# A recurrent attention block and a maxout FFN in one kernel: query and score parts of y made transposed from the fifth chunk on, one weight load for keys and queries in odd units

## The chip, the core and the metric

One core of one Trainium2 chip runs the whole program. The metric is the device time of one execution in microseconds. Before the change three runs took 515.86, 516.76 and 520.91 us; the median is 516.76.

## What is computed

Two blocks follow each other. The first is a delta rule, a recurrence over 768 tokens with a 48x48 state for each of 4 batches and 8 heads; the second is a feed-forward network (FFN) with a maximum over three products. Cut to what matters:

```python
q, k, v: (4, 8, 768, 48); beta: (4, 8, 768)
k_n = k / (norm(k) + 1e-6)
for t in range(768):
    y[:, :, t] = q[t] @ state
    v_old = state.T @ k_n[t]
    state = state + beta[t] * outer(k_n[t], v[t] - v_old)
x = y.transpose(0, 2, 1, 3).reshape(3072, 384)
h = maximum(maximum(x @ w1, x @ w2), x @ w3)      # w: (384, 768)
out = h @ w_out                                   # (768, 384)
```

## The kernel before

**Tiles.** The 768 tokens are cut into 12 chunks of 64. A chunk has two units (g = 0, 1), each with two of the four batches; unit n belongs to chunk n // 2. Within a unit the two batches (bb) stand on partitions 0 to 63 and 64 to 127. Two chunks of all four batches make 512 tokens, one FFN group m (0 to 5). Everything is fp32, and the trace has two records for each such matmul.

**A chunk's steps.** For each unit `gram` (L395) multiplies the transposed keys with the keys (`at`) and with the queries (`pt`, masked to the causal part). The score matrix of 64x64 needs a triangular solve; `solve` (L498) does it for 32-token blocks of two chunks at once, on VectorE, with a round trip through DRAM (`at_d`, `x_bl`, `y_d`, `ut`); `join_z` and `join_u` put the halves together. Then `old_k` (L738) subtracts keys times state from the values (`p_k`), `new` (L753) applies the solved triangle (`p_u`, copied to `u` by ScalarE), `step` (L771) adds to the state (`p_s`, `st`), `old_q` (L747) makes queries times state (`p_q`, copied to `qs` by ScalarE) and `to_y` (L793) adds the scores times `u` (`p_y`) on VectorE. Every one of these small products is 32 matmuls on the four 64x64 quadrants of TensorE, so 64 records.

**From y to x.** The FFN needs x with its 384 features on partitions. For chunks 0 to 3 `to_x` (L807) transposes y on TensorE. For chunks 4 to 11 `y_blocks` (L833) writes y to DRAM by two transfers from SP's queue, `read_y` (L844) reads it back into the tile `qall` by four, with another order, and `turn_y` (L857) turns 32x32 blocks on VectorE into `xt`.

**The order is written out by hand.** `ffn(m)` (L903) is a generator that yields after each product. At its yields the loop at the end (L1173) issues steps of the recurrence for group m + 1 and loads for later groups, by a table of names and digits:

```python
LINKS = {
    0: "k0 q0 t0 L3", 1: "t1", 2: "g0 g1 t2", 3: "z0 z1 d0 d1", 4: "j0 j1 t3 V0",
    5: "g2 g3 p1", 6: "u0 N0", 7: "V1 N1", 8: "s0 y0 N2", 9: "x0", 10: "k1 q1",
    11: "u1 w0", 13: "y1 x1 s1", 14: "X0 w1", 16: "P0", 17: "X1 K0 K1 K2 K3",
}
```

Digits 0 and 1 of k, q, u, s, y, x, w and X name the even and the odd chunk of the group. A yield of the first twelve is one hidden product (`p_h`, 3 matmuls); from yield 12 on it is half an output product (`p_o`). So the recurrence of chunks 4 to 11 is made within passes 1 to 4 over the FFN. The first pass, m = 0, has a table of its own (`FIRST`, `EARLY_LINKS`) with chunks 1 to 3 in it, the units 8 to 11 of `gram`, and the conversion of the weights (`mant`, `up` on ScalarE, VectorE and POOL). The solve of group m + 2 begins at yield 8 of pass m, for m up to 3, and goes on in small portions, three steps a yield. Each engine works through its own queue in the order recorded; a step that waits holds up what stands behind it on that engine.

**PSUM.** `p_h`, `p_m` and `p_o` take turns in two buffers (`ffn`), all the small products in three buffers of two banks (`two`). A p_h stage of yield i can begin when the buffer of yield i - 2 is read: by ScalarE's ReLU for the even yields, by VectorE's maximum (L928) for the odd ones.

Of the kernel before, what the change touches and what calls it, by code (L numbers as in the profile page):

```python
# [9 lines left out]
FP32 = mybir.dt.float32  # L10
# [4 lines left out]
ALU = mybir.AluOpType  # L15

C = 64
# [6 lines left out]
def kernel(  # L24
# [31 lines left out]
    nc = tc.nc  # L56

    B, H, S, D = q.shape
    NCH = S // C
    DM = H * D  # L60
    DFF = moe_w1.shape[1]
    KT = DM // 128
    FT = DFF // 128
    NP = H // 2
# [18 lines left out]
    def ps_two(name):  # L83
        return psum.tile([128, 2, 512], FP32, name=name, tag="two", bufs=3)
# [5 lines left out]
    qall = const.tile([128, NQ, H, DP], FP32, name="qall")  # L90
# [18 lines left out]
    def rows(bb):  # L109
        return slice(C * bb, C * (bb + 1))  # L110

    def dims(par):
        return slice(DP * par, DP * par + D)
# [196 lines left out]
    def by_par(t):  # L310
        return t.rearrange("p (j two) x -> p two j x", two=2)
# [83 lines left out]
    def gram(n, parts=(0, 1), queues=one_queue, copy=nc.scalar.copy, later=False):  # L395
        kqt, g = kqts[n], n % 2
        p_g = ps_two("p_g")

        whole = len(parts) == 2 and not g
        for j in range(NP):  # L400
            for par in range(2):
                for bb in range(2):
                    kq = kqt[dims(par), j, bb ^ g]
                    for i in (0,) if whole else parts:
                        c0 = j * 128 + i * C
                        nc.tensor.matmul(  # L406
                            p_g[
                                rows(bb ^ (g * i)), par, c0 : c0 + C * (1 + whole)
                            ],
                            kq[:, 0],  # L410
                            kq if whole else kq[:, i],
                        )
        p_v = p_g.rearrange("p two (j i t) -> p two j i t", j=NP, i=2)
        if 1 in parts:
            pt = pts[n] = square("pt")
            if later:
                copy(by_par(pt), p_v[:, :, :, 1])
            else:
                masked(pt, p_v[:, :, :, 1])
        if 0 not in parts:  # L420
            return
        at = ats[n] = square("at")
        copy(by_par(at), p_v[:, :, :, 0])
        if queues:
            to_dram(n, queues)
# [178 lines left out]
    def both(name, w, bufs=1):  # L604
        return work.tile([128, 2, H, w], FP32, name=name, bufs=bufs)
# [110 lines left out]
                negate[bb](u12[block(bb), :, span(hs)], p_v[bb][block(bb)], -1.0)  # L716


    xts, rhss, qss, us, yts = {}, {}, {}, {}, {}

    def heads(t):
        return t.rearrange("p g (j two) d -> p two (g j) d", two=2)

    def times_state(kqt, i, name):
        p_b = ps_two(name)
        for j in range(NP):
            for g in range(2):
                for par in range(2):
                    for bb in range(2):
                        c0 = (g * NP + j) * D  # L730
                        nc.tensor.matmul(  # L731
                            p_b[rows(bb), par, c0 : c0 + D],
                            kqt[g][dims(par), j, bb ^ g, i],
                            st[dims(par), bb ^ g, g, j],
                        )
        return p_b[:, :, 0 : H * D].rearrange("p two (x d) -> p two x d", d=D)

    def old_k(c):  # L738
        rhss[c] = vts.pop(c)
        if c:  # L740
# [3 lines left out]
                out=rhs, in0=rhs, in1=times_state(kqt, 0, "p_k"), op=ALU.subtract  # L744
            )

    def old_q(c):  # L747
        kqt = [kqts[2 * c + g] for g in range(2)]
        if c:
            qs = qss[c] = both("qs", D)  # L750
            nc.scalar.copy(heads(qs), times_state(kqt, 1, "p_q"))

    def new(c):  # L753
        rhs = rhss.pop(c)
# [38 lines left out]
    def to_y(c):  # L793
        u = us[c]
        pt = [pts.pop(2 * c + g) for g in range(2)]
        y = yts[c] = both("y", D)
        for hs, p_v, copy in heads_of(c, "p_y", D):
            for i, h in enumerate(hs):
                for bb, g in TILES:
                    r = rows(bb ^ g)  # L800
                    nc.tensor.matmul(p_v[rows(bb), g, i], pt[g][r, h], u[r, g, h])  # L801
            if c:
                nc.vector.tensor_tensor(out=y, in0=qss.pop(c), in1=p_v, op=ALU.add)
            else:
                copy(y[:, :, span(hs)], p_v)

# [21 lines left out]
        if c:  # L828
            nc.scalar.copy(xt, of)

    yds, yqs = {}, {}

    def y_blocks(c):  # L833


        y = yts.pop(c)
        y_d = yds[c] = dram.tile([32, 2, 4, DM], FP32, name="y_x")
        for g in range(2):
            nc.sync.dma_start(
                out=y_d[:, g].rearrange("t b x -> b t x"),  # L840
                in_=y[:, g].rearrange("p h d -> p (h d)"),
            )

    def read_y(c):  # L844
        y_d = yds.pop(c)
        y_q = yqs[c] = qall.rearrange("p i h d -> p (i h d)")[
            :, 768 * (c % 2) : 768 * (c % 2 + 1)
        ].rearrange("p (b x) -> p b x", x=96)
        for a in range(4):
            nc.sync.dma_start(  # L850
                out=y_q[32 * a : 32 * (a + 1)],
                in_=y_d[:, :, :, 96 * a : 96 * (a + 1)].rearrange(
                    "t g b x -> t (g b) x"
                ),
            )

    def turn_y(c):  # L857
        m, cc = divmod(c, 2)
        if m not in xts:
            xts[m] = work.tile([128, KT, TOK], FP32, name="xt")  # L860
        nc.vector.transpose(
            out=xts[m][:, :, cc * 256 : (cc + 1) * 256].rearrange(
                "p t (b x) -> p b t x", x=32
            ),
            in_=yqs.pop(c).rearrange("p b (x t) -> p b t x", t=KT),
        )

    def less_first(f):
# [34 lines left out]
    def ffn(m):  # L903
        xt = xts[m]
        hs = {}

        def hidden(f, lo, w):
            if f not in hs:
                hs[f] = square("h").rearrange("p h c -> p (h c)")
            h = hs[f][:, lo : lo + w]  # L910
            for i in range(m > 0, 3):
                p_h = ps_ffn([128, TOK], "p_h")[:, 0:w]
                for t in range(KT):
                    nc.tensor.matmul(  # L914
                        p_h,
                        w_sb[i][:, t, f * 128 : (f + 1) * 128],
                        xt[:, t, lo : lo + w],
                        start=(t == 0),
                        stop=(t == KT - 1),
                    )  # L920
                if i == 0:
                    nc.scalar.copy(h, p_h)
                elif m and i == 1:
                    nc.scalar.activation(  # L924
                        out=h, in_=p_h, func=mybir.ActivationFunctionType.Relu
                    )
                else:
                    nc.vector.tensor_tensor(out=h, in0=h, in1=p_h, op=ALU.max)  # L928
                yield


        early = FT // 2 if m == 0 else 0
        for lo in (0, TOK // 2):
            for f in range(early):
                yield from hidden(f, lo, TOK // 2)
        for f in range(early, FT):
            yield from hidden(f, 0, TOK)
        for i in range(4):
            cc, g = divmod(i, 2)
            p_o = ps_ffn([128, DM], "p_o")  # L940
            last = slice(i * 128, (i + 1) * 128)
            terms = [(hs[f][:, last], wo_sb[:, f]) for f in range(FT)]
            if m:
                terms += [(xt[:, t, last], w_sb[0][:, t, 0:DM]) for t in range(KT)]
            for n, (stays, moves) in enumerate(terms):
                nc.tensor.matmul(  # L946
                    p_o, stays, moves, start=(n == 0), stop=(n == len(terms) - 1)
                )
                if m and n == 4:
                    yield  # L950
            o_sb = work.tile([128, DM], FP32, name="o_sb")
            nc.scalar.copy(o_sb, p_o)  # L952
            for bb in range(2):
                tok0 = (2 * bb + g) * S + (2 * m + cc) * C
                nc.sync.dma_start(out=out[tok0 : tok0 + C, :], in_=o_sb[rows(bb)])
            yield


# [79 lines left out]
    for _ in range(2):  # L1038
# [25 lines left out]
    LINKS = {  # L1064
# [3 lines left out]
    }  # L1068
    EARLY_LINKS = {
# [11 lines left out]


    RECURS = dict(
        z=join_z, j=join_u, k=old_k, q=old_q, u=new, s=step, y=to_y, x=to_x,
        e=halves_z, f=halves_u, d=turn_t1,
    )
    MADE = dict(V=load_v, P=prep_values)
# [79 lines left out]
            turn_first((2 * (i - 27), 2 * (i - 27) + 1))  # L1167


    RECURS.update(x=y_blocks, w=read_y, X=turn_y, p=prep_values)  # L1170
    UNIT.update(t=turn_blocks, K=lambda n: load_k(n, (nc.gpsimd, nc.gpsimd)))
    MADE.update(V=lambda c: load_v(c, nc.gpsimd))
    for m in range(1, GROUPS):  # L1173
# [42 lines left out]
```

## Time and profile before

The profiled execution took 523.32 us (span from first to last instruction 521.3 us, mean granted TensorE clock 0.966), against the median of 516.76 us of the three runs.

| what (line) | engine | count | mean |
|---|---|---|---|
| p_h, 128x512 (L914) | TensorE | 414 records | 606 ns, overlapped |
| y addition, 128x768 (L803) | VectorE | 11 | 952 ns |
| state addition, 48x768 (L789) | VectorE | 14 | 951 ns |
| 128x1024 product of the solve (L538) | VectorE | 4 | 1224 ns |
| mask of pt, 128x512 (L390) | VectorE | 20 | 689 ns |
| transpose to xt, 128x768 (L861) | VectorE | 8 | 1224 ns |
| copy of p_q, 128x768 (L751) | ScalarE | 11 | 800 ns |
| copy of 128x1024 from PSUM (L335) | ScalarE | 4 | 1009 ns |
| y to DRAM (L839) | SP's queue | 16 | 192 KB each |
| y back from DRAM (L850) | SP's queue | 32 | 96 KB each, 2.6 us to landing |

Matmuls overlap in their pipeline, so a stage's time is read from its start to the start of the next stage, not from the means of its records. "Idle before, with a releaser" names what ended an engine's wait. Passes over the FFN begin at 46, 162, 246, 322, 395 and 463 us.

### The profile page before, as it was taken

The numbers are of one execution on the slowest core, as the hardware profiler recorded it, in microseconds if no ns is written. First come the engines' busy times: TensorE is split into PE (matmuls) and PEld (weight loads), VectorE is DVE, ScalarE is ACT, GpSimd is POOL, SyncE is SP. The second block draws the span as 40 slices with busy tenths as digits, with TensorE's granted clock in tenths as the row PEclk, the third lists the DMA queues.
The fourth block names the chain that finished last, engine by engine and source line by source line (L and its number), as shares of the span: only waits on it lengthen the run. The fifth ranks groups of instructions, "written<-read, shape, count | busy, mean of one in ns | idle before, by whom it ended". The sixth has DMA issues, their size and how long they took to land.

```text
span 521.3 us, 18005 instructions
## 1 busy us (share of the span) xinstructions
PE 496.0 (95%) x7836; PEld 306.0 (59%) x7836; DVE 306.0 (59%) x689; ACT 163.3 (31%) x302; POOL 192.6 (37%) x317
## 2 busy tenths in 40 slices
PE   7578799998999999999999999999999999999996
PEld 6467688755565555665555565555655555654453
DVE  5888969867996430998642987635896321111100
ACT  4575755883422242201243101252101411011000
POOL 6435462783391926670665680503130000000000
PEclk9956989999999999999989999999999999999999
DMA  8927969764055925353675354823343202220011
GB/s 116 205 37 208 209 136 149 189 192 106 2 132 141 180 49 130 102 129 84 148 126 123 107 144 95 169 38 92 83 106 83 41 3 63 62 60 0 0 30 30
DMA packets 105277, 53.45 MB, mean 103 GB/s; under 512 B 89712, under 2 KB 98960, under 8 KB 105200
## 3 DMA queue, kind: packets, MB, share of 16 engines
q1 hardware_dynamic: 93616, 31.55, 30.0%
q0 software_dynamic: 9472, 20.37, 15.9%
q8 instruction: 61, 1.00, 0.8%
q10 hardware_dynamic: 2112, 0.39, 0.5%
q14 instruction: 16, 0.13, 0.1%
HBM read 39.17 MB, written 13.11 MB: 100 GB/s over the span
## 4 chain that ended last, share of the span: by engine, by line
PE 80%; DMA 7%; DVE 6%; ACT 2%; issue 2%; SPq 2%; POOL 1%; DVEq 0%; ACTq 0%; POOLq 0%
PE p_h L914 35%; PE p_o L946 26%; PE p_g L406 2%; PE p_u L759 2%; PE p_m L894 2%; PE p_k L731 2%; PE p_q L731 2%; PE p_y L801 2%; DMA kmore<-in_k_dram 2%; PE p_s L782 2%; PE p_j L714 2%; DMA x_bl<-at_d 2%; DMA qall<-in_q_dram 1%; DMA ut<-y_d 1%; SPq L120 1%
## 5 line engine op out<-in xcount | busy, mean ns | idle before, releaser
L914 PE MATMUL p_h<-xt,w_sb 128*128 128x512 f32 (+1 forms) x522 | 220.7, 567 | 1.9 <-issue 1.2
L914 PEld LDWEIGHTS p_h<-xt,w_sb 128*128 128x128 f32 x522 | 96.6, 194 | 88.2 <-issue 81.1
L946 PE MATMUL p_o<-wo_sb,h 128*128 128x384 f32 x288 | 97.7, 489 | 0.0
L928 DVE TENSOR_TENSOR h<-h,p_h 128x512 f32<-128x512 f32 (+1 forms) x48 | 29.6, 617 | 93.6 <-PE p_h L914 93.0
L946 PEld LDWEIGHTS p_o<-wo_sb,h 128*128 128x128 f32 x288 | 53.7, 190 | 35.7 <-issue 0.5
L552 DVE TENSOR_TENSOR tmp<-x_bl,y_bl 128x31 f32<-128x31 f32 (+20 forms) x139 | 51.4, 370 | 4.1
L952 ACT COPY o_sb<-p_o 128x384 f32<-128x384 f32 x24 | 11.5, 479 | 132.1 <-PE p_o L946 126.0
L556 DVE TENSOR_TENSOR y_bl<-y_bl,tmp 128x31 f32<-128x31 f32 (+20 forms) x139 | 48.5, 349 | 4.8
L924 ACT ACTIVATE h<-p_h 128x512 f32<-128x512 f32 x30 | 17.9, 597 | 90.3 <-PE p_h L914 87.3
L946 PE MATMUL p_o<-w_sb,xt 128*128 128x384 f32 x120 | 42.0, 486 | 0.0
L364 POOL DMA_DIRECT2D turned<-in_q_dram x72 | 39.3, 554 | 5.4 <-POOL turned L359 3.1
L254 POOL TENSOR_TENSOR w_sb<-mant,up 128x384 int32<-128x384 int32 x18 | 18.8, 1046 | 41.1 <-DVE mant L250 39.0
L946 PEld LDWEIGHTS p_o<-w_sb,xt 128*128 128x128 f32 x120 | 22.8, 190 | 15.9
L406 PEld LDWEIGHTS p_g<-kqt 48*64 48x64 f32 x1216 | 24.3, 141 | 9.9 <-issue 6.4
L406 PE MATMUL p_g<-kqt 48*64 48x64 f32 (+1 forms) x1216 | 27.5, 240 | 0.9 <-ACT kqt L335 0.8
L120 POOL DMA_DIRECT2D kpad<-in_k_dram x32 | 21.9, 692 | 13.8 <-issue 12.7
L789 DVE TENSOR_TENSOR st<-st,p_s 48x768 f32<-48x768 f32 (+1 forms) x18 | 17.1, 950 | 15.3 <-PE p_s L782 15.1
L139 POOL DMA_DIRECT2D v_t<-in_v_dram x14 | 11.6, 832 | 38.1 <-PE p_u L759 38.1
L390 DVE TENSOR_TENSOR pt<-p_g,mask 128x512 f32<-128x512 f32 x20 | 13.8, 689 | 16.1 <-PE p_g L406 15.8
L287 POOL TENSOR_TENSOR v_t<-v_t,nrm 128x768 f32<-128x768 f32 x12 | 17.9, 1495 | 9.0 <-DVE nrm L281 8.9
L359 POOL MEMSET turned<- 128x96 f32 x18 | 3.3, 192 | 46.6 <-DVE kqt L380 46.6
L759 PEld LDWEIGHTS p_u<-v_t,ut 64*64 64x64 f32 x768 | 14.2, 149 | 8.9 <-issue 6.4
(143 smaller groups left out, 616.4 us busy)
## 6 DMA issues: line engine op xcount, KB each, us to landing
out_dram<-o_sb SPq DMA_DIRECT2D x48, 96.0 KB, 2.2
w_bits<-in_moe_w_dram SPq DMA_DIRECT2D x9, 384.0 KB, 6.0
w_bits<-in_moe_w_dram POOLq DMA_DIRECT2D x9, 384.0 KB, 5.6
turned<-in_q_dram POOLq DMA_DIRECT2D x72, 48.0 KB, 2.8
kpad<-in_k_dram POOLq DMA_DIRECT2D x32, 96.0 KB, 5.9
y_x<-y SPq DMA_DIRECT2D x16, 192.0 KB
qall<-y_x SPq DMA_DIRECT2D x32, 96.0 KB, 2.6
v_t<-in_v_dram POOLq DMA_DIRECT2D x14, 192.0 KB, 4.8
```

Of the source, the lines that this page charges most:

```text
L120: queues[bb].dma_start(out=dst[rows(bb ^ g), :, 0:D], in_=src[2 * bb + g, :, c * C : (c + 1) * C, :].rearrange("h p d -> p h d"),)
L254: nc.gpsimd.tensor_tensor(out=dst.bitcast(I32), in0=mant_v.bitcast(I32), in1=up_v, op=ALU.add)
L287: nc.gpsimd.tensor_tensor(out=vts[c], in0=vts[c], in1=nrm[:, :, :, None].to_broadcast([128, 2, H, D]), op=ALU.mult,)
L364: (queue, nc.gpsimd)[i].dma_start(out=t[p0 : p0 + 32, bb, at : at + NP * 2 * D].rearrange("p (j x) -> p j x", j=NP), in_=(k, q)[i][2 * bb ...
L406: nc.tensor.matmul(p_g[rows(bb ^ (g * i)), par, c0 : c0 + C * (1 + whole)], kq[:, 0], kq if whole else kq[:, i],)
L552: nc.vector.tensor_tensor(out=t_v, in0=row.to_broadcast(t_v.shape), in1=column.to_broadcast(t_v.shape), op=ALU.mult,)
L556: nc.vector.tensor_tensor(out=rest, in0=rest, in1=t_v, op=ALU.subtract)
L731: nc.tensor.matmul(p_b[rows(bb), par, c0 : c0 + D], kqt[g][dims(par), j, bb ^ g, i], st[dims(par), bb ^ g, g, j],)
L759: nc.tensor.matmul(p_v[rows(bb ^ g), g, i], ut[c % NU][rows(bb), g, h], rhs[rows(bb), g, h],)
L914: nc.tensor.matmul(p_h, w_sb[i][:, t, f * 128 : (f + 1) * 128], xt[:, t, lo : lo + w], start=(t == 0), stop=(t == KT - 1),)
L928: nc.vector.tensor_tensor(out=h, in0=h, in1=p_h, op=ALU.max)
L946: nc.tensor.matmul(p_o, stays, moves, start=(n == 0), stop=(n == len(terms) - 1))
```

## The change

1. `gram` uses one load of a key block for keys and queries in the odd units too (all units from 8 on): 16 matmuls with 128 moving columns in place of 32 with 64. The query scores of an odd unit then come out on the other half of the partitions, and VectorE's mask moves them over, in two instructions of 64 partitions in place of one of 128.
2. From chunk 4 on (`OVER = 4`), `old_q` and `to_y` make their products transposed: the state, or `u`, is the stationary operand (48 columns) and the queries, or scores, move (64 columns). The results have the 48 features on partitions, at 0 to 47 and 64 to 111, and 1024 numbers a partition. ScalarE copies them in two instructions of 48 partitions, VectorE adds in two. They lie in a part of `qall`, which all these chunks share.
3. `y_out` writes this y to DRAM by two transfers of 48x8x128 numbers, and `x_in` reads x from there by one transfer directly into `xt`. The VectorE transposes are gone. In the table X0 and X1 are gone, and w1 moves from yield 14 to yield 15.
4. For chunks 1 to 3 y is added in place, into the tile that holds the query part, so one buffer of the tag `y` serves both.
5. The output rows of a tile belong to other batches for these chunks, so the addresses of the writes follow.

```diff
-        whole = len(parts) == 2 and not g
+        whole = len(parts) == 2
...
-            if later:
+            if whole and g:
+                for bb in range(2):
+                    nc.vector.tensor_tensor(
+                        out=by_par(pt)[rows(1 - bb)], in0=p_v[rows(bb), :, :, 1],
+                        in1=mask[rows(bb), None, None, :].to_broadcast([C, 2, NP, C]),
+                        op=ALU.mult,
+                    )
+            elif later:
...
+    OVER = 4
...
+    def y_tile(c):
+        if c >= OVER:
+            t = qall.rearrange("p i h d -> p (i h d)")[:, 0 : 2 * H * C]
+            return t.rearrange("p (h x t) -> p h x t", h=H, x=2)
+        return both("y", D)
+
+    def over(bb):
+        return slice(C * bb, C * bb + D)
...
-        if c:
-            qs = qss[c] = both("qs", D)
+        if 0 < c < OVER:
+            qs = qss[c] = y_tile(c)
             nc.scalar.copy(heads(qs), times_state(kqt, 1, "p_q"))
+        elif c:
+            p_q = ps_two("p_q").rearrange("p two (j x t) -> p two j x t", x=2, t=C)
+            for j in range(NP):
+                for g in range(2):
+                    for par in range(2):
+                        for bb in range(2):
+                            nc.tensor.matmul(
+                                p_q[over(bb), par, j, bb ^ g],
+                                st[dims(par), bb ^ g, g, j],
+                                kqt[g][dims(par), j, bb ^ g, 1],
+                            )
+            qs = qss[c] = y_tile(c)
+            for bb in range(2):
+                nc.scalar.copy(
+                    by_par(qs[over(bb)].rearrange("p h x t -> p h (x t)")),
+                    p_q[over(bb)].rearrange("p two j x t -> p two j (x t)"),
+                )
...
-        y = yts[c] = both("y", D)
+        y = yts[c] = qss.pop(c) if c else y_tile(c)
+        if c >= OVER:
+            p_y = ps_two("p_y").rearrange("p x (h t) -> p x h t", h=H)
+            for h in range(H):
+                for bb, g in TILES:
+                    r = rows(bb ^ g)
+                    nc.tensor.matmul(
+                        p_y[over(bb), bb ^ g, h], u[r, g, h], pt[g][r, h]
+                    )
+            for bb in range(2):
+                part = y[over(bb)].rearrange("p h x t -> p x h t")
+                nc.vector.tensor_tensor(
+                    out=part, in0=part, in1=p_y[over(bb)], op=ALU.add
+                )
+            return
...
-                nc.vector.tensor_tensor(out=y, in0=qss.pop(c), in1=p_v, op=ALU.add)
+                nc.vector.tensor_tensor(out=y, in0=y, in1=p_v, op=ALU.add)
...
-    def y_blocks(c):
+    def y_out(c):
         y = yts.pop(c)
-        y_d = yds[c] = dram.tile([32, 2, 4, DM], FP32, name="y_x")
-        for g in range(2):
+        y_d = yds[c] = dram.tile([H, D, 2, 128], FP32, name="y_x")
+        for bb in range(2):
             nc.sync.dma_start(
-                out=y_d[:, g].rearrange("t b x -> b t x"),
-                in_=y[:, g].rearrange("p h d -> p (h d)"),
+                out=y_d[:, :, bb].rearrange("h d x -> d h x"),
+                in_=y[over(bb)].rearrange("d h x t -> d h (x t)"),
             )
-    def read_y(c):
...
-    def turn_y(c):
...
+    def x_in(c):
         m, cc = divmod(c, 2)
         if m not in xts:
             xts[m] = work.tile([128, KT, TOK], FP32, name="xt")
+        nc.sync.dma_start(
+            out=xts[m][:, :, cc * 256 : (cc + 1) * 256],
+            in_=yds.pop(c).rearrange("h d b x -> (h d) (b x)").rearrange(
+                "(p t) x -> p t x", t=KT
             ),
         )
...
-        11: "u1 w0", 13: "y1 x1 s1", 14: "X0 w1", 16: "P0", 17: "X1 K0 K1 K2 K3",
+        11: "u1 w0", 13: "y1 x1 s1", 15: "w1", 16: "P0", 17: "K0 K1 K2 K3",
```

More of the change, by code (lines that the diff above doesn't have):

```diff
@@ L829, in to_x @@
             nc.scalar.copy(xt, of)
-    yds, yqs = {}, {}
-    def y_blocks(c):
+    yds = {}
+    def y_out(c):
         y = yts.pop(c)
-        y_d = yds[c] = dram.tile([32, 2, 4, DM], FP32, name="y_x")
-        for g in range(2):
+        y_d = yds[c] = dram.tile([H, D, 2, 128], FP32, name="y_x")
+        for bb in range(2):
             nc.sync.dma_start(
-                out=y_d[:, g].rearrange("t b x -> b t x"),
-                in_=y[:, g].rearrange("p h d -> p (h d)"),
-            )
-    def read_y(c):
[L845 to L855, printed above, removed]
-    def turn_y(c):
+                out=y_d[:, :, bb].rearrange("h d x -> d h x"),
+                in_=y[over(bb)].rearrange("d h x t -> d h (x t)"),
+            )
+    def x_in(c):
         m, cc = divmod(c, 2)
@@ L860, in turn_y @@
             xts[m] = work.tile([128, KT, TOK], FP32, name="xt")
-        nc.vector.transpose(
-            out=xts[m][:, :, cc * 256 : (cc + 1) * 256].rearrange(
-                "p t (b x) -> p b t x", x=32
+        nc.sync.dma_start(
+            out=xts[m][:, :, cc * 256 : (cc + 1) * 256],
+            in_=yds.pop(c).rearrange("h d b x -> (h d) (b x)").rearrange(
+                "(p t) x -> p t x", t=KT
             ),
-            in_=yqs.pop(c).rearrange("p b (x t) -> p b t x", t=KT),
         )
@@ L938, in ffn @@
         for i in range(4):
-            cc, g = divmod(i, 2)
+            cc, part = divmod(i, 2)
             p_o = ps_ffn([128, DM], "p_o")
@@ L952, in ffn @@
             nc.scalar.copy(o_sb, p_o)
-            for bb in range(2):
-                tok0 = (2 * bb + g) * S + (2 * m + cc) * C
-                nc.sync.dma_start(out=out[tok0 : tok0 + C, :], in_=o_sb[rows(bb)])
+            for other in range(2):
+                b = 2 * part + (part ^ other) if 2 * m + cc >= OVER else 2 * other + part
+                tok0 = b * S + (2 * m + cc) * C
+                nc.sync.dma_start(out=out[tok0 : tok0 + C, :], in_=o_sb[rows(other)])
             yield
@@ L1083 @@
     RECURS = dict(
-        z=join_z, j=join_u, k=old_k, q=old_q, u=new, s=step, y=to_y, x=to_x,
+        z=join_z, j=join_u, k=old_k, q=old_q, u=new, s=step, y=to_y, w=x_in,
+        x=lambda c: y_out(c) if c >= OVER else to_x(c),
         e=halves_z, f=halves_u, d=turn_t1,
@@ L1167 @@
             turn_first((2 * (i - 27), 2 * (i - 27) + 1))
-    RECURS.update(x=y_blocks, w=read_y, X=turn_y, p=prep_values)
+    RECURS.update(p=prep_values)
     UNIT.update(t=turn_blocks, K=lambda n: load_k(n, (nc.gpsimd, nc.gpsimd)))
```

## The prediction

> **What bounds the kernel now.** I read the busy shares first, then the chain of work that ended last, then each FFN pass in the order of time.
>
> ```profile
> PE 496.0 (95%) x7836; PEld 306.0 (59%) x7836; DVE 306.0 (59%) x689; ACT 163.3 (31%) x302; POOL 192.6 (37%) x317
> PE 80%; DMA 7%; DVE 6%; ACT 2%; issue 2%; SPq 2%; POOL 1%; DVEq 0%; ACTq 0%; POOLq 0%
> ```
>
> TensorE is busy in every slice from 162 us on, which is where all of the transposed path lies: chunks 4 to 11, made inside FFN passes 1 to 4 (162 to 246, to 322, to 395, to 463 us). So an edit counts there by what it does to TensorE's own time, or by a wait that TensorE gets or loses; VectorE, ScalarE and SP count only through such a wait. The chain of pass 3 shows the one place where it leaves TensorE for VectorE:
>
> ```profile
> 356.52 0.94 PE p_s L782 x64
> ...
> 357.49 0.95 DVE st L789
> ...
> 358.46 0.96 DVE st L789
> ...
> 359.45 0.95 DVE y L803
> ...
> 363.90 1.22 DVE x_bl L538
> 365.13 0.61 DVE h L928
> ...
> 365.78 2.84 PE p_h L914 x6
> ```
>
> There the even chunk's state and y additions stand in VectorE's queue ahead of the start of the next solve and of one h maximum; that maximum (of the first p_h stage after p_y) frees the PSUM buffer for the third such stage. TensorE has just run out of other work, so the slack is about 0.05 us. The same pair (end of h, start of that p_h) is 216.73 and 217.15 in pass 1, 292.57 and 292.98 in pass 2: slack 0.42 and 0.41. Pass 4 has no solve and a slack of some us. The order of time at the start of pass 2 shows the other wait:
>
> ```profile
> 263.33 0.72 PE L701 MATMUL p_z<-ut,at 32*32 32x32 f32 x60 [1.18 <-DMA ut<-y_d]
> 263.98 4.54 PE L914 MATMUL p_h<-xt,w_sb 128*128 128x512 f32 x6
> ```
>
> TensorE waits 1.18 us for the solve's result, and the six p_h records behind it take 4.54 us instead of 2.8: the granted clock from 262 to 272 is 0.83, some 1.7 us lost. In pass 0, ScalarE waits for the y addition of chunk 2 before it copies chunk 3's query part:
>
> ```profile
> 135.32 0.80 ACT L751 COPY qs<-p_q 128x768 f32<-128x768 f32 x1 [4.70 <-DVE y L803]
> 138.97 1.15 PE L782 MATMUL p_s<-u,kmore 64*64 64x48 f32 x64
> ```
>
> **What the skill says.** (1) The Trainium skill, "TensorE: Matmul & The Clock Gate", section "LDWEIGHTS (loading the stationary operand)": loading costs by columns, not rows. The trace agrees for quadrant work: p_s with 48 stationary columns takes 0.76 us from its start to the next stage's, p_k with 64 takes 0.96, both with 48 moving. (2) The same page, Part 1: TensorE falls to half its clock after an idle window of about 3.4 us. The trace is harsher: 1.18 us beside 2 us of 32x32 work was enough at 262, while gaps of 1.24 us at 55 and 1.33 at 126 cost no clock. (3) "DMA: Bandwidth & Descriptors", section "Why a DMA increments its semaphore by 16 and not by 1": a transfer uses the largest number of engines up to 16 that divides the slowest dimension of both sides. The old y_x write has 4 (batch) there; the trace shows 4 of 16 engines:
>
> ```profile
> 449.50:450.00 0.50, 0.50 (x3) 1.00 0.27 98
> 450.00:450.50 0.50, 0.50 (x3) 1.00 0.27 101
> ```
>
> (DMA share 0.27, 98 GB/s.) The new one has 48 on both sides, so 16 engines, by the page. (4) "VectorE: DVE Perf Modes", section "Mode 1× (REGULAR) — the baseline": one fp32 result a cycle for tensor_tensor. The trace agrees, and partitions don't matter: 48x768 takes 951 ns, 128x768 952.
>
> **The change, part by part.**
>
> Gram, 8 odd units (9 to 23): 16 matmuls of 128 columns in place of 32 of 64. In pass 2 the even unit takes 0.94 us (29.4 ns for each of 32 records) and the odd one 0.97 (15.2 ns for each of 64), by the records in 0.1 us stretches. So the stream bounds the wide form and halving the loads gains 8 × 0.03 = **-0.2 us** (bounds ±0.8). VectorE gets one more mask each, 0.69 us: 5.5 in all. In passes 1 to 3 the next h waits 0.80 and more for TensorE, which hides it; in pass 0 the masks fall beside POOL's 1.49 us scale, which blocks VectorE's following `mant` anyway, and beside POOL's own queue at 105.5. I take **+0.2** (0 to +1.4 if neither cover holds).
>
> p_q and p_y, 16 stages: the same number of matmuls, with 48 stationary and 64 moving columns for 64 and 48. Not in the trace. From below the p_s price (48 and 48): 0.20 less each, -3.2; from above 64 and 64: 0.97 against 0.96, and +1.0 if some are worse. The stream bound seen above for 128 columns halves to 0.94 for 64, so I take **-0.5**.
>
> ScalarE: eight times two 48x1024 copies for one 128x768. The 128x1024 copies take 1.01 to 1.04 us: 2 × 1.02 - 0.80 = 1.24 more each. Behind them stands the u copy; in pass 3 it ends at 370.6 and p_y needs it at 375.6. Hidden. Of odd chunks these copies also wait until the even chunk's y has left `qall`. The old write landed 5.6 to 8.3 us after its issue; with 16 engines I expect 3 to 4, so about 292.5 in pass 2, before p_q is done at 293. Hidden, with 3 us in reserve at u.
>
> VectorE: two 48x1024 additions (1.22 us each, the price of the 128x1024 row L538) for one of 0.95: **1.48 more** per chunk. The even chunk's stands ahead of the h maximum: 1.48 less the slacks 0.42, 0.41 and 0.05 makes TensorE wait 1.06 + 1.07 + 1.43 = **+3.6**. The odd chunk's is paid by the two removed transposes (1.22 each, and a wait of 0.65 in pass 1).
>
> End of the solve: in pass 1 VectorE runs without a gap, so y_d leaves 1.48 + 1.48 - 2.44 - 0.65 = 0.13 us earlier, while TensorE comes 1.06 later: **-1.1** of the 1.18 wait. The half clock behind it may go too: -1.7 or 0, taken **-0.85**. At the start of pass 4 p_z takes 1.59 us for 1.28; y_d gains about 1 us on TensorE: **-0.3**.
>
> The shared y tile of chunks 1 to 3: chunk 3's query copy is recorded before chunk 2's y is transposed, and both now lie in one buffer. So the copy waits for p_x, at 136.45 instead of 135.3; behind it are three weight conversions, an h copy and the u copy (end 138.73 to 139.86), and p_s, ready at 138.97, waits: **+0.9** (0.5 to 1.2).
>
> SP and the x path: per chunk 2 writes and 1 read for 2 and 4, so about 1.9 us less issue (0.61 each). Before, the odd chunk's path from addition to xt took 15.3 us (229.4 to 244.7) and had 1.7 to spare; now 1.5 more addition, about 3 less for the write, one landing of some 4 us in place of 2.5 issue, 2.6 landing and 1.2 transpose. No worse. The output rows only change places.
>
> New gaps: four of about 1 us beside quadrant work. Of the gaps listed, some cost the clock 1.7 us and some nothing; I take one: **+1.7**.
>
> Sum: -0.2 + 0.2 - 0.5 + 3.6 - 1.1 - 0.85 - 0.3 + 0.9 + 1.7 = **+3.5 us**. The profiled execution took 523.32 us (span 521.3), 6.6 over the median of 516.76; on its own account that is 526.8, on the median's **520.3**.
>
> **Rivals.**
> (a) Load-bound quadrants: the 48-column price holds (-3.2 for -0.5), no new gap costs clock and the old half clock goes (-0.85 more): 3.5 - 2.7 - 1.7 - 0.85 = -1.8, so 515.0. For it: p_s against p_k. Against: the wide Gram form is bound by its stream.
> (b) A slower end: the y write lands as late as before, or later for its 512-byte pieces. Then ScalarE stands before the odd chunk's copies, the u copy behind it is late, and TensorE waits at p_y. It decides from about 3 us beyond the times above (landing 8 us after the addition); each us more costs 4, since four passes have it, and x for the next pass, with 1.7 to spare, is late too. At 2 us beyond, 8 with the sum: 528. Against: 4 engines now.
> (c) Every new gap drops the clock and the old one stays: 3.5 + 5.1 + 0.85 = +9.5, 526.
> (d) The additions do not delay TensorE (a slack that I misread): 3.5 - 3.6 - 1.7 + 1.1 = -0.7, 516.
>
> **How the numbers follow.** Forecast 0.50 (517 to 523), (a) 0.18, (b) 0.10, (c) 0.12, (d) 0.10. A run of this kernel tells about 1% (5.2 us) from no change. Slower by more than 1% is (b), (c) and about a third of the forecast: 0.38. Faster takes (a) with more than it promises: 0.07. The rest, 0.55, is within 1%. The range leaves out the far ends of (b) and (c) and the low end of (a): 515.0 to 526.0.
>
> **What would show it.** In the changed profile: the third p_h stage after the even p_y in passes 1 to 3 starts 1 to 1.5 us late, right behind VectorE's h; p_q and p_y take 0.9 to 1.0 us each; p_g pairs stay near 2.0; ScalarE's chunk 3 copy stands for p_x; no `ut` wait at the start of pass 2; DMA share well over 0.27 while y is written. Wrong if ScalarE waits for y_x, if p_h of a pass waits for xt, or if p_q falls to 0.76.

## The result, and the profile after

The changed kernel takes 521.29 us (median of 11 runs, 519.08 to 523.93), the kernel before in the same session 517.47 (11 runs, 515.86 to 520.91): ratio 1.0088, 95% interval 1.0063 to 1.0112. It is slower by 3.8 us. The prediction was 520.3, from 515.0 to 526.0.

The two profiled executions say something else at first sight: 523.32 us before, 523.55 after. The profiled execution of the kernel before was a slow one: its 523.32 us lie above all of its 11 runs. So one pair of profiles can't be subtracted here, and the first experiment is a second profile of each. The busy shares and the chain by engine of the changed kernel:

```profile
PE 494.8 (95%) x7580; PEld 303.9 (58%) x7580; DVE 316.3 (61%) x697; ACT 172.3 (33%) x310; POOL 192.9 (37%) x317
...
PE 73%; DVE 13%; DMA 4%; ACT 3%; issue 2%; POOL 1%; SPq 1%; DVEq 0%; ACTq 0%; POOLq 0%
```

TensorE is still the busiest. Its 1.2 us less isn't less work: the profile of before has stretches at a lower clock in it, and the second profiles give 494.4 us before and 494.0 after. VectorE has 10.3 us more, and its share of the chain went from 6% to 13%: the chain now runs through it in three passes. The chain of pass 3 in the changed kernel (start, duration, what):

```profile
354.82 0.94 PE p_s L816 x64
...
355.78 0.94 DVE st L823
...
356.76 0.96 DVE st L823
...
357.75 1.21 DVE qall L841
...
358.99 1.23 DVE qall L841
...
364.01 0.60 ACT h L959
...
364.65 2.84 PE p_h L949 x6
367.49 0.65 issue
368.14 1.26 PE p_u L793 x64
```

The two additions of y now stand where one of 0.95 us stood. The chain comes back to TensorE by a ReLU of ScalarE, and then TensorE stands still once more, 0.65 us ahead of p_u. The idle time of TensorE in passes 1 and 3 (timeline of TensorE; idle time before the instruction and its releaser in brackets):

```profile
217.16 2.84 PE L949 MATMUL p_h<-xt,w_sb 128*128 128x512 f32 x6 [0.22 <-ACT h L959]
220.66 1.15 PE L793 MATMUL p_u<-v_t,ut 64*64 64x48 f32 x64 [0.65 <-issue]
...
364.65 2.84 PE L949 MATMUL p_h<-xt,w_sb 128*128 128x512 f32 x6 [0.74 <-ACT h L959]
```

"issue" means that the view found no releaser. VectorE's timeline of the changed kernel in pass 1 gives one:

```profile
217.60 0.69 DVE L963 TENSOR_TENSOR h<-h,p_h 128x512 f32<-128x512 f32 x1
...
219.61 0.94 DVE L751 TENSOR_TENSOR v_t<-v_t,p_k 128x768 f32<-128x768 f32 x1
```

p_u needs v_t less p_k. The subtraction ends at 220.55, p_u starts at 220.66; in passes 2 and 3 too p_u starts 0.10 us behind it. It stands in VectorE's queue behind the solve's first steps and the h maximum. In the kernel before there was room here (VectorE, then TensorE, pass 1):

```profile
218.05 0.95 DVE L743 TENSOR_TENSOR v_t<-v_t,p_k 128x768 f32<-128x768 f32 x1
```

```profile
219.92 1.15 PE L759 MATMUL p_u<-v_t,ut 64*64 64x48 f32 x64
```

The subtraction ended 0.92 us ahead of p_u. ScalarE shows the other half of the changed kernel's delay:

```profile
216.40 0.25 ACT L534 COPY y_bl<-bl 128x32 f32<-128x32 f32 x1 [6.92 <-DVE bl L532]
216.52 0.59 ACT L959 ACTIVATE h<-p_h 128x512 f32<-128x512 f32 x1
217.01 2.04 ACT L782 COPY qall<-p_q 48x1024 f32<-48x1024 f32 x2
```

The third p_h stage now gets the PSUM buffer of the second, which a ReLU empties: it starts at 217.16, ahead of the maximum at 217.60 that empties the first stage's. That ReLU stands behind the solve's diagonal copy, and this copy waits 6.92 us for VectorE. So VectorE's queue delays TensorE through two other doors than the one the prediction watched.

### The profile page after: what moved, and what is told of

Its sections match the earlier page's. It is cut to its first block, busy times and chain, and to the rows that moved or that the text cites. A ratio compares the mean times of both kernels' runs of the same rounds, so it can differ in the third digit from the quotient of the medians.

```text
span 520.4 us, 17482 instructions
## 1 busy us (share of the span) xinstructions
PE 494.8 (95%) x7580; PEld 303.9 (58%) x7580; DVE 316.3 (61%) x697; ACT 172.3 (33%) x310; POOL 192.9 (37%) x317
## 4 chain that ended last, share of the span: by engine, by line
PE 73%; DVE 13%; DMA 4%; ACT 3%; issue 2%; POOL 1%; SPq 1%; DVEq 0%; ACTq 0%; POOLq 0%
PE p_h L949 31%; PE p_o L981 25%; PE p_g L406 3%; PE p_m L929 2%; DVE tmp L559 2%; PE p_u L793 2%; DMA kmore<-in_k_dram 2%; PE p_s L816 2%; DVE st L823 1%; PE p_k L739 1%; DMA qall<-in_q_dram 1%; DVE qall L841 1%; PE p_j L721 1%; SPq L120 1%; PE p_z L708 1%
## 5 line engine op out<-in xcount | busy, mean ns | idle before, releaser
L949 PE MATMUL p_h<-xt,w_sb 128*128 128x512 f32 (+1 forms) x522 | 218.4, 563 | 1.7 <-ACT h L959 1.2
L559 DVE TENSOR_TENSOR tmp<-x_bl,y_bl 128x31 f32<-128x31 f32 (+20 forms) x139 | 53.5, 385 | 4.3
L406 PEld LDWEIGHTS p_g<-kqt 48*64 48x64 f32 x960 | 23.0, 145 | 9.3 <-issue 7.0
L406 PE MATMUL p_g<-kqt 48*64 48x128 f32 (+1 forms) x960 | 27.0, 262 | 0.9 <-ACT kqt L335 0.8
L841 DVE TENSOR_TENSOR qall<-qall,p_y 48x1024 f32<-48x1024 f32 x16 | 19.5, 1218 | 9.1 <-PE p_y L836 8.7
L430 ACT COPY at<-p_g 128x512 f32<-128x512 f32 x22 | 12.8, 585 | 22.5 <-DVE pt L390 13.5
```

What stands on the lines that cost most here:

```text
L406: nc.tensor.matmul(p_g[rows(bb ^ (g * i)), par, c0 : c0 + C * (1 + whole)], kq[:, 0], kq if whole else kq[:, i],)
L559: nc.vector.tensor_tensor(out=t_v, in0=row.to_broadcast(t_v.shape), in1=column.to_broadcast(t_v.shape), op=ALU.mult,)
L841: nc.vector.tensor_tensor(out=part, in0=part, in1=p_y[over(bb)], op=ALU.add)
L949: nc.tensor.matmul(p_h, w_sb[i][:, t, f * 128 : (f + 1) * 128], xt[:, t, lo : lo + w], start=(t == 0), stop=(t == KT - 1),)
```

## The experiments

Theory: what the change costs is the 1.48 us that VectorE takes longer between p_s and p_u of the odd chunk in passes 1 to 3, some 3.5 us in all, and 0.9 us for the shared y tile in pass 0. Rivals: the quadrant stages of TensorE, the granted clock, the Gram edit, or a mishap of single executions.

Three measures serve for all runs. The ratio is that of the medians, to the kernel before in the same session; the sessions were on different chips, so ratios of different sessions compare less well than those of one. "Rest" is the time from the first p_k of pass 1 to the end of the chain, from one profile; it leaves out pass 0, whose length differs by some us between profiles of one kernel (that p_k starts at 161.80 in one profile of the kernel before and at 164.87 in the other). The last column is the time on TensorE from the start of the even chunk's p_s to the start of the odd chunk's p_s, in passes 1, 2 and 3: the stretch in which the theory puts the loss.

| run | ratio, 95% interval | rest, us | p_s to p_s, us |
|---|---|---|---|
| before, first profile | 1 | 352.74 | 19.98, 19.98, 20.15 |
| e1_before_again | one execution | 349.72 | 19.98, 19.98, 20.15 |
| changed | 1.0088 (1.0063 to 1.0112) | 352.66 | 21.20, 20.99, 21.51 |
| e11_changed_again | one execution | 352.38 | 21.29, 20.98, 21.52 |
| e2_gram_alone | 1.0019 (0.9996 to 1.0042) | 348.69 | 19.98, 19.98, 20.14 |
| e6_gram_from_12 | 1.0028 (1.0007 to 1.0049) | 350.51 | 19.98, 19.98, 20.20 |
| e8_changed_without_gram | 1.0065 (1.0043 to 1.0087) | 352.65 | 21.06, 21.00, 21.52 |
| e3_own_tiles | 1.0076 (1.0047 to 1.0105) | 352.48 | 21.30, 20.98, 21.52 |
| e5_before_more_vector | 1.0068 (1.0048 to 1.0089) | 353.39 | 20.84, 20.82, 21.36 |
| e4_even_y_late | 1.0103 (1.0074 to 1.0131) | 351.80 | 20.64, 20.72, 21.03 |
| e7_late_more_squares | 1.0020 (0.9997 to 1.0043) | 348.80 | 19.86, 19.87, 19.91 |
| e9_combined | 1.0026 (1.0003 to 1.0048) | 349.18 | 19.87, 19.87, 19.91 |
| e10_combined_gram | 1.0018 (0.9999 to 1.0037) | 348.81 | 19.87, 19.87, 19.92 |

**Both kernels again.** No edit.

> The kernel before, unchanged, for a second profile of it. In the profile at hand its passes from the first p_h on took 84.2, 75.9, 72.8 and 67.8 us, and the wait for ut at the start of pass 2 came with some 1.7 us of lower clock. If that wait and its clock drop belong to the kernel, pass 1 and pass 2 come out again within 0.5 us of 84.2 and 75.9. If the drop is chance of one execution, pass 2 is 73.5 to 74.5, which would put the kernel before some 1.5 to 2.5 us lower than its own profile showed, and would account for most of the difference between equal profiles (523.3 and 523.6) and unequal medians (517.5 and 521.3).

> The changed kernel, unchanged, for a second profile of it. The idle stretches ahead of the third p_h stage (0.22, 0.22, 0.74 us) and of p_u (0.65 three times) belong to its order and come again within 0.05; passes 2 to 4 take 73.4, 73.9 and 67.2 again. The idle 0.56 us within p_j of pass 1 has no releaser: if it comes at the same place it belongs to the program, if not to the execution, and pass 1 is then 85.3 for 86.0.

The chain of the kernel before, second profile, at the start of pass 2:

```profile
258.18 1.28 PE p_z L701 x98
259.46 2.77 PE p_h L914 x6
```

The same profile by stretches of time (the third number from the end is the granted clock):

```profile
258.00:272.00 14.00, 14.00 (x431) 8.60 (x433) 6.72 (x14) 7.01 (x12) 8.27 (x16) 1.00 0.57 105
```

No wait for ut, no lower clock: the 1.18 us and the lower clock behind it (0.57 from 264 to 268), which the first profile showed, belong to that one execution. From 64 us on the clock is 1.00 in every stretch of 10 us of the twelve other profiles, but for one of 0.99. A wait for ut comes in other places in other runs: 0.61 us in e5, 0.51 in e6, 0.53 in e9. Pass 2 takes 72.58 us (from p_k to p_k) where the first profile had 75.85; passes 1 and 3 repeat within 0.05. The rest is 3.0 us shorter, more than the 1.5 to 2.5 expected. The idle stretches of the changed kernel at p_h and p_u come back to 0.01 us. So the clean comparison is 349.72 against 352.66 or 352.38, +2.7 to +2.9, and the loss lies in the last column: 1.22 + 1.01 + 1.36 = 3.6 us.

**More work on VectorE in the kernel before.**

```diff
                 nc.vector.tensor_tensor(out=y, in0=qss.pop(c), in1=p_v, op=ALU.add)
+                if c in (4, 6, 8):
+                    for r in (y[0:48], y[0:48, 0]):
+                        nc.vector.tensor_tensor(out=r, in0=r, in1=r, op=ALU.max)
```

> The kernel before with 1.45 us more work on VectorE right behind the even chunk's y addition of passes 1 to 3 (two maxima of y with itself, 48x768 and 48x384; the values stay), everything else as before. Theory (VectorE's queue from p_s to the third p_h stage has no room): passes 1 to 3, which took 84.2, 72.6 and 72.8 us in the kernel before, become 1.0, 1.0 and 1.4 us longer, 3.4 in all, the fourth stays at 67.9: 520.4, ratio 1.0066. Rival (the changed kernel's loss is due to its buffers and ScalarE's copies, not to VectorE's time): passes unchanged within 0.3, ratio 1.000.

Ratio 1.0068 where 1.0066 was expected. The stretch grows by 0.86, 0.84 and 1.21 us: 2.9 where 3.4 was expected and the change makes 3.6. In pass 3 the waits are those of the changed kernel, the p_h behind a ReLU among them (timeline of TensorE); in passes 1 and 2 only p_u shows idle time, 0.53 and 0.52.

```profile
363.26 2.84 PE L917 MATMUL p_h<-xt,w_sb 128*128 128x512 f32 x6 [0.61 <-ACT h L927]
366.62 1.26 PE L759 MATMUL p_u<-v_t,ut 64*64 64x48 f32 x64 [0.52 <-issue]
```

Time on VectorE alone, at this place, makes the kernel before lose nearly what the change loses. This run also waited 0.61 us for ut at the start of pass 3, so not all of the ratio is the stretch, and its nearness to 1.0066 is in part luck.

**The even chunk's y behind p_u.**

```diff
+            if c % 2:
+                t = work.tile([128, 2 * H * C], FP32, name="y_odd", bufs=1)
...
-11: "u1 w0", 13: "y1 x1 s1",
+11: "u1 y0 x0", 13: "y1 x1 s1 w0",
```

(y0 leaves link 8 and x0 link 9; the odd chunk's q and y get a tile of their own, because the even y is still in `qall` when the odd query stage is copied.)

> The changed kernel with the even chunk's p_y and its two additions moved from beside p_s to behind p_u of the odd chunk, so that they stand in VectorE's queue behind the start of the solve, two h maxima and the subtraction from v_t; the odd chunk's y has a tile of its own so that its query copies wait for nothing. Theory (VectorE's queue delays the third p_h stage and p_u by 1.15, 1.0 and 1.55 us in passes 1 to 3): 3.5 us faster than the changed kernel, 517.8, ratio to before 1.000 to 1.002, no idle time ahead of p_h or p_u near 217, 290 and 364. Rival (the time is TensorE's own: quadrant stages dearer, or clock): ratio stays at 1.007 to 1.009. Rival (the additions delay something else further on, as the second p_o group or the end of the solve): ratio 1.004 to 1.009 with a new wait behind p_u.

It came out no faster, 1.0103. The p_h and p_u stalls are gone from passes 1 and 2 (in pass 3 0.32 us is left ahead of p_h), but a new one stands ahead of p_o in all three (timeline of TensorE, then of ScalarE, pass 1):

```profile
222.03 4.14 PE L984 MATMUL p_o<-wo_sb,h 128*128 128x384 f32 x12 [0.70 <-ACT h L962]
```

```profile
221.38 0.60 ACT L962 ACTIVATE h<-p_h 128x512 f32<-128x512 f32 x1 [6.70 <-PE p_y L839]
```

A ReLU waits for p_y: its h tile comes from the pool that pt shares, and the buffer it gets is a pt that the delayed p_y still reads. The experiment removed one wait and made another. Its rest is 0.9 us shorter than the changed kernel's, which its ratio doesn't show; why is left open. The next run mends the pool (edit against e4).

```diff
-        return work.tile([128, H, C], FP32, name=name, tag="square", bufs=17)
+        return work.tile([128, H, C], FP32, name=name, tag="square", bufs=18)
...
-        return both("y", D)
+        t = work.tile([128, 2 * H * C], FP32, name="y_odd", bufs=1)
+        return t[:, 0 : 2 * H * D].rearrange("p (g h d) -> p g h d", g=2, h=H)
```

> The changed kernel with the even chunk's y behind p_u as in the run e4_even_y_late, and one buffer more (18 for 17) in the pool that h, pt and at share; y of chunks 0 to 3 lies in the odd chunk's tile. In that run one ReLU waited for p_y to be done with a pt buffer, and the first p_o for that ReLU: 0.70 us in each of three passes. Theory: with the extra buffer that wait goes too, no pass has an idle stretch of TensorE over 0.3 us, passes 1 to 3 come to 84.2, 72.4 and 72.6 us with the Gram gain, and the time to 518 to 519, ratio 1.001 to 1.004 (the shared tile and pass 0 are left). Rival (the pool hands out another buffer in use): the idle stretch shows at another stage, ratio 1.006 to 1.010.

1.0020: of 1.0088, 0.0068 or 3.5 us are gone. The third p_h stage and p_u follow without a wait (timeline of TensorE, pass 2):

```profile
289.45 2.84 PE L953 MATMUL p_h<-xt,w_sb 128*128 128x512 f32 x6
292.22 1.15 PE L797 MATMUL p_u<-v_t,ut 64*64 64x48 f32 x64
```

From pass 1 on TensorE has one idle stretch left, 0.17 us at the start of pass 3. The stretch p_s to p_s is 0.12, 0.11 and 0.24 us shorter than in the kernel before. In passes 1 and 2 that is TensorE's own gain from the transposed stages, visible once the queue of VectorE no longer covers it; in pass 3 it is also the small wait that the kernel before had there (its p_q took 1.21 us to the start of p_h, for 1.05 and 1.04 in passes 1 and 2). ScalarE's two longer copies are still in this run, so they aren't the cause. Together with the opposite experiment this settles the main term.

**The shared y tile.** Query part and y of chunks 1 to 3 in two tiles again.

```diff
-            qs = qss[c] = y_tile(c)
+            qs = qss[c] = both("qs", D)
             nc.scalar.copy(heads(qs), times_state(kqt, 1, "p_q"))
...
-                nc.vector.tensor_tensor(out=y, in0=y, in1=p_v, op=ALU.add)
+                nc.vector.tensor_tensor(out=y, in0=qs, in1=p_v, op=ALU.add)
```

> The changed kernel with two tiles again for query part and y of chunks 1 to 3 (the transposed path from chunk 4 on stays). Theory: chunk 3's query copy no longer waits for the transposes of chunk 2, p_s of chunk 3 no longer waits for u, 0.9 us less: 520.4, ratio to before 1.007, and the ACT u wait of p_s near 138 us is gone. Rival: the 0.9 us is made up before the pass ends, 521.3, ratio 1.009.

TensorE in pass 0, changed kernel, then this run:

```profile
132.68 1.15 PE L793 MATMUL p_u<-v_t,ut 64*64 64x48 f32 x64
...
138.17 1.15 PE L816 MATMUL p_s<-u,kmore 64*64 64x48 f32 x64 [0.88 <-ACT u L798]
```

```profile
136.20 1.15 PE L816 MATMUL p_s<-u,kmore 64*64 64x48 f32 x64
```

The wait of 0.88 us is gone. From p_k to p_s of this chunk the changed kernel takes 12.66 us (12.64 in e11), this run 11.82, the kernel before 11.33 and 10.91. The ratio is 0.0012 or 0.6 us below the changed kernel's, with intervals (6 runs for this one) that neither confirm nor refute 0.9. The other kernels that keep the shared tile show the same wait, 0.88 to 0.90.

**The Gram edit.** Alone on the kernel before, then from unit 12 on only (shown against the first of these), then taken out of the changed kernel.

```diff
-        whole = len(parts) == 2
+        whole = len(parts) == 2 and (not g or n >= 12)
```

> The kernel before with the Gram edit alone: odd units load the keys once, and mask in two halves. Theory of the changed trace (p_g pair 1.91 us for 2.02, eight pairs): 0.9 us faster, 516.6, ratio 0.998. Theory of the prediction (stream bound): 0.0, ratio 1.000. Rival, that the added mask of 0.69 us on VectorE delays TensorE in passes 1 to 3 as the y additions are held to do: slower by up to 2 us, ratio 1.002 to 1.004.

> The kernel before with the Gram edit from unit 12 on only, so in passes 1 to 3 and not in pass 0. The edit in all units gave 1.0 us less from the start of pass 1 on, and yet a ratio of 1.0019 (0.9996 to 1.0042). Theory (its two extra masks in pass 0, where VectorE leads the chain, cost 1 to 2 us): 0.9 us faster than before, ratio 0.998, and 1.5 to 2 us faster than the edit in all units. Rival (the ratio above 1 was chance): no difference to the edit in all units beyond 0.5 us, both near 0.999 to 1.000.

> The changed kernel with the old Gram products of odd units. Theory (the Gram edit saves 0.11 us a pair from pass 1 on and loses 1 to 2 us by masks in pass 0): 0 to 1 us faster than the changed kernel, 520.3 to 521.3, with passes 1 to 4 together 1.0 longer and pass 0 shorter. Rival (it only saves): 1.0 us slower, 522.3, ratio 1.011. The stalls at p_h and p_u of passes 1 to 3 stay in both.

A p_g stage of two units takes 1.91 us for 2.02, so the two stages of each of passes 1 to 3 save 0.66 us, and e2's rest is the shortest of all. Its p_s to p_s is that of the kernel before, so the rival that the masks hold up TensorE there falls. Yet no comparison shows a gain in the time: 1.0019, 1.0028, and 1.0065 without the edit against 1.0088 with it; only e10 against e9 leans the other way (1.0018 against 1.0026), and the intervals overlap. e8's rest, expected 1.0 us longer than the changed kernel's, is as long. The theory that the masks cost time in pass 0 finds no support: without them there e6 is no better. What takes the gain back isn't settled.

Two idle stretches of TensorE without a releaser go with the edit. One is in pass 0. In all six profiles that have the edit from unit 8 on and p_q ahead of p_u (changed, e11, e2, e3, e4, e7) TensorE stands still for 0.85 to 1.32 us ahead of the last 7 records of chunk 3's p_q; in the five without it there (both of before, e5, e6, e8), and in e10, where p_q stands behind p_u, it doesn't. Changed kernel, then e8:

```profile
129.65 0.33 PE L739 MATMUL p_q<-st,kqt 48*64 48x48 f32 x7 [1.21 <-issue]
```

```profile
129.05 1.15 PE L786 MATMUL p_u<-v_t,ut 64*64 64x48 f32 x64 [0.75 <-DVE v_t L744]
```

Where the gap is missing p_u mostly waits for the subtraction instead, so the gap costs less than its length: from p_k to p_s of this chunk e8 takes 12.05 us, the changed kernel 12.66 and 12.64. It may be part of what takes the gain back; e6, which hasn't got it and gains nothing either, says that it isn't all. The other stretch, inside p_j, is from pass 1 on in six of eight profiles with the edit and in none of five without. In the changed kernel and in its second profile:

```profile
185.85 0.39 PE L721 MATMUL p_j<-z,t 32*32 32x32 f32 x24 [0.56 <-issue]
```

```profile
266.49 0.98 PE L721 MATMUL p_j<-z,t 32*32 32x32 f32 x69 [0.21 <-issue]
```

This one changes its pass from execution to execution, so it is no fixed wait of the program. In pass 0 kernels without the edit have such a stretch in p_j as well (2.21 us in the first profile of before, 0.45 in e1), so the edit isn't needed for it. The cause of neither was tried.

**All put together.** Even y late with 18 buffers, the old Gram, and in pass 0:

```diff
-        23: "k1 y0 q1", 24: "u1 x0",
+        23: "k1 y0", 24: "u1 x0 q1",
```

> The transposed path with three things put right: the even chunk's y behind p_u with the 18th buffer (as in e7_late_more_squares), the old Gram products of odd units, and in pass 0 the query stage of chunk 3 recorded behind the transposes of chunk 2 and the u stage, so that its copy into the shared tile stands in front of nothing. Theory: against e7_late_more_squares (ratio 1.002) the shared tile gives back 0.9 us and the Gram edit about 1, so 516.5, ratio 0.998, with p_s of chunk 3 no longer waiting for u; from the start of pass 1 on about as the kernel before (0.9 less for that run, 0.9 more without the Gram edit). Rival (nothing is left of the transposed path's own gain): ratio 1.000 to 1.002.

> The run e9_combined with the Gram edit as well. Its stages get 0.11 us a pair shorter, 0.9 in all. If that reaches the time: ratio 0.996. If, as the two runs of the Gram edit on the kernel before showed (1.0019 and 1.0028), something takes it back, ratio 0.999 to 1.001, and the profile should show where: an idle stretch of TensorE within p_j (seen in four of six profiles with the edit and in none of four without), or a wait for ut.

Neither beats the kernel before: 1.0026 and 1.0018, both a little above every ratio that was named for them. The reordering in pass 0 doesn't give the 0.9 us back. p_s no longer waits for u, but p_u now waits for the subtraction (timeline of TensorE, e9):

```profile
129.97 1.15 PE L790 MATMUL p_u<-v_t,ut 64*64 64x48 f32 x64 [1.39 <-DVE v_t L744]
```

p_q had filled part of that wait. From p_k to p_s of chunk 3 this run takes 12.05 us, as long as e8, which has the old order and the old Gram products too.

## Why the prediction came out right, step by step

**VectorE's additions** (+3.6: 1.06, 1.07, 1.43): right in size, 1.22, 1.01 and 1.36 (e11: 1.31, 1.00, 1.37). Wrong in place: the prediction put the whole wait at the third p_h stage behind VectorE's h. There, behind a ReLU, only 0.24, 0.25 and 0.61 us are lost (p_q from its start to that of p_h, against the kernel before); 0.72 or 0.73 more are lost ahead of p_u each time, and 0.11 in p_u's stage in passes 2 and 3 or 0.32 at the first p_o in pass 1. The prediction named no wait of p_u, which had 0.92 us of reserve, and read its slacks from one wait; the delay reached TensorE at the next consumers of the same queue. That the sum held is in part luck, since this reserve isn't the 0.42 of the p_h stage. VectorE's price also held: 1218 ns for 48x1024 against 951 for 48x768, so 1.04 ns for each of the 256 further columns. That agrees with the Trainium skill, "VectorE: DVE Perf Modes", section "Mode 1× (REGULAR) — the baseline", by which the results come one a cycle.

**End of the solve** (-1.1, -0.85, -0.3) **and new gaps** (+1.7): wrong. The prediction took the wait for ut and its half clock, seen in one execution, for a property of the kernel, and credited the change with removing them; e1 shows the kernel before without them. Only the term of pass 4 is real: p_z takes 1.28 us there for 1.59 in the first profile of before, and for 1.83 in e1, with a wait of 0.32 shown. Against that it charged one clock drop for the new gaps; none came, the granted clock is 1.00 in the stretches around them, with gaps of 0.2 to 0.75 us. The two errors, -2.0 and +1.7, cancel by luck. On its own account, where the first profile's accident counts in full, the sum gave 526.8 and the profile 523.55; only on the medians was it near.

**Shared y tile** (+0.9): 0.88 to 0.90 in the trace. **p_q and p_y** (-0.5): p_q 0.90 for 0.93, p_y 0.90 and 1.04 for 0.93 and 1.08, 0.13 a pass, -0.5 in four. The low bound of 0.76, which the prediction took from p_s, was not met: p_y with the same 48 stationary columns takes 0.93 us ahead of a p_s stage, and p_s itself 0.86 ahead of p_h (e7). So rival (a) falls, though its other half, that no new gap costs the clock, held.

**Gram** (-0.2, masks +0.2): the stages save more than predicted, 0.11 a pair for 0.03; the time saves nothing. The wide form was held to be bound by its stream, and it wasn't wholly.

**Left out:** the idle stretch in p_j. From p_k to the even p_s pass 1 takes 43.79 us with it and 43.01 without (e11), +0.8; in e11 it is in pass 2, 31.76 for 31.37, +0.4.

**ScalarE, SP and the x path** (nothing): right. ScalarE's copies from chunk 4 on wait for p_q alone. SP's wait for the y write fell from 53.6 us in all (10 waits) to this (list of SP's waits: us in total, times, longest):

```profile
SPq L896 <- DMA y_x<-qall: 10.9, 4, 3.7
```

The DMA share while y is written is 0.56 to 0.90 for 0.27; the low end, in pass 4 (clock, DMA share and GB/s are the last three numbers):

```profile
447.50:448.00 0.50, 0.50 (x3) 0.25 (x2) 0.00 (x0) 0.00 (x0) 0.00 (x0) 1.00 0.56 119
```

So more than 4 of 16 engines work. That agrees with the Trainium skill, "DMA: Bandwidth & Descriptors", section "Why a DMA increments its semaphore by 16 and not by 1": 48 rows on both sides where 4 batches stood. Rival (b) falls. So do (c), since no clock was lost, and (d), by e5 and e7.

Summed again from pass 1 on, start to start on TensorE, the changed kernel's first profile against e1: p_s to p_s +3.6, with a gain of the stages of about 0.12 a pass in it; from p_k to the even p_s +0.6, -0.2 and -0.3, which is the stretch in p_j less 0.2 a pass for p_g; pass 4 -0.7, of it 0.55 for p_z and 0.13 for p_q and p_y. That makes the +2.9 measured. For pass 0 the medians, which differ by 3.8, leave 0.9. The wait for u of 0.88 fits, but pass 0 holds the gap in p_q as well, and its length differs by 3 us between profiles, so this share is argued and not shown.

## What to carry to other kernels

Price a longer operation by what stands behind it in its engine's queue, down to the next point where the bounding engine meets that queue, not at the first wait alone: a pool that hands out its buffers in another order can move the wait to another instruction. Before a wait or a clock drop of one profile is credited to a change, look whether a second profile of the same kernel has it. When an operation is moved away from a crowded queue, follow the buffers that it holds longer; here the move alone gained nothing (1.0103), and with one buffer more in a pool it gained 3.5 us (1.0020).

## What was not expected of the hardware

The stretch from p_s to p_s repeats within 0.06 us over four profiles of the kernel before and its Gram variants, while pass 0 of one and the same kernel differs by 3 us from profile to profile. So a stretch of stages tells a change of 0.2 us where the whole time doesn't; where the spread of the runs comes from was not tried. And the length of a gap alone did not decide the clock here: 1.18 us beside 32x32 work was followed once by 0.57, while 1.39 us ahead of p_u in e9 and 1.49 us within p_s in e7, both in pass 0 beside quadrant work, left it at 1.00. The Trainium skill, "TensorE: Matmul & The Clock Gate", Part 1, names an idle window of about 3.4 us; no gap of these profiles from 46 us on is that long, so the loss behind 1.18 us stays without an explanation.
